# Attention bias made by distance, and full-height value weights, in a fused attention and expert kernel

## The chip, the cores and the metric

One core of a Trainium2 chip runs the whole program. The metric is device time in microseconds (us), a median over runs. PE is the matrix engine (TensorE), DVE VectorE, ACT ScalarE, POOL GpSimd, SP the engine that issues most DMAs.

## The reference, cut to what matters

```
scores = scale * q @ k^T                                  # 2 batches, 8 heads, 576 x 576, head_dim 64
psi_rel = log1p(|i - j|);  psi_i = log1p(max(i, 1))
x = psi_rel / psi_i
bias[h, i, j] = relu(x * w1 + b1) @ w2                    # 32 hidden units, 8 heads
attn = softmax(scores + bias)
x = attn @ v                                              # then reshaped to 1152 tokens x 512
x = sum_e p[e] * relu(x @ moe_w1[e]) @ moe_w2[e]          # 4 experts, 1024 wide
h = x @ w_in;  g = (a0+a1 h+a2 h^2+a3 h^3) / (1+|b0||h|+|b1|h^2 + 1e-6);  out = g @ w_out
```

For a given row i the bias depends on j only through |i - j|. All data are float32; a product is made from rounded high and low parts (the `h` and `l` tiles).

## The kernel before, in words

The program has three stages on one core: the bias (about 0 to 64 us), attention (to about 217 us), and the two expert stages. Within a stage, engines run their own queues in order and wait for each other on semaphores. DMA semaphores come in eight lanes, so a DMA waits for the one eight places ahead of it.

**Bias, `bias_phase`.** 36 groups `gg` of 16 rows each. A group has four tiles `q`; each is 128 partitions (4 rows x 32 hidden units) by 576 columns j. `hidden` (L402) makes each tile from a table of logarithms `ltab` (shifted by the row) and a per-partition constant `shift`: one instruction on DVE (L416) or ACT (L413), as `HIDDEN` says: "DDDA", three on DVE and one on ACT, 108 and 36 in all. `products` (L420) multiplies them on PE with `wm` in 32-column strips, two halves of 288 columns, into a PSUM tile `ps_ab` (3 buffers). `combine` (L436) divides by psi_i while it copies the PSUM tile on ACT into `bo` (L442), of which a tile holds a band of four groups (2 buffers); `store` (L426) writes a band to DRAM `bias_d`. `load_bias` (L492) reads 128 rows of two heads back for attention. Hidden tiles have 16 slots, four groups' worth, and run LEAD = 2 groups ahead of the products.

Between the groups stand other pieces: POOL splits k, q and v of head pair 0 into high and low (`split_hi` L527, `split_lo` L532) at the start, and k of the next at group 22; SP loads the next raw tiles behind the splits that free them; PE transposes k and q (`qk_T`, L548); at groups 34 and 35 the first two blocks of scores (L594) are already made.

**Attention.** Eight units n (head pair, batch), nine score blocks each. The order of all five queues is written by a small planner (`Flow`) from a table of costs and offsets (`CFG`). Per block: scores on PE (L594), bias and minimum on DVE (L608), exponent on ACT (L616), division on POOL (`norm`, L636), transposes on PE (L653, L666, L669), high and low copies on ACT and DVE (L678, L682). Per unit and half (256 or 320 rows) and head, `av` (L701) multiplies the transposed weights with v: for e = 0 to 3 a chunk of 128 keys, for e = 4 the last 64 keys. Both heads' last 64 keys lie in one v chunk and one tile `pe`, one head in partitions 0 to 63 and the other in 64 to 127, so e = 4 is a product over 64 partitions:

```
r = slice(64 * h, 64 * h + 64)
lh, rh = vs[r, 4].rearrange("p a d -> p (a d)"), el_[r, :W]
nc.tensor.matmul(ps[:, :W], lhsT=lh, rhs=rh, start=(e == 0 and m is mh), stop=(e == 4 and m is ml))
```

`pt_tiles` takes the weight tiles `pt` and `pe` from two buffers of 320 columns in turn, one half after the other.

Of the kernel before, what the change touches and what calls it, by code (L numbers as in the profile page):

```python
# [24 lines left out]
P = 128  # L25
# [14 lines left out]

NTQ, NDT = S // 4, 1148
LEAD = 2
# [3 lines left out]
EARLY = {34: (0,), 35: (1,)}  # L46
HIDDEN = ["DDDA"] * (S // 16)
OUT_DVE = ()

# [85 lines left out]
class Kernel:  # L135
# [16 lines left out]
    def run(self):  # L152
# [5 lines left out]
        self.dram = ctx.enter_context(self.pool("dscr", DRAM))  # L158
        self.bias_d = [self.dram.tile([P, H, S] if c < 4 else [16, H, 4, S], F32, name=f"bias_d{c}") for c in range(5)]
        self.nc.scalar.preload_act_table_set("natural_log_exp_and_others")  # L160
# [211 lines left out]


    def bias_phase(self):
        nc, t, pa = self.nc, self.t, self.pa
        cw = pa.tile([P, 10], F32, name="cw")
        mask = pa.tile([P, 4], F32, name="mask")
        shift = pa.tile([P, NTQ], F32, name="shift")
        rpsi = pa.tile([P, S // 16], F32, name="rpsi")
        ltab = pa.tile([P, NDT], F32, name="ltab")  # L380
        nc.sync.dma_start(out=cw, in_=t["w1_b1_w2"])
        nc.scalar.dma_start(out=shift, in_=t["c_psi"])
        for i, (a, b) in enumerate(((NDT - 640, NDT), (0, NDT - 640))):
            nc.sync.dma_start(out=ltab[:, a:b], in_=t["c_ltab"][:, a:b])
# [8 lines left out]
        nc.vector.tensor_scalar(out=shift, in0=shift, scalar1=b1, scalar2=None, op0=ALU.mult)  # L393
        nc.vector.tensor_scalar(out=ltab[:, NDT - 640:NDT], in0=ltab[:, NDT - 640:NDT], scalar1=w1, scalar2=None, op0=ALU.mult)
        wm = pa.tile([P, 4, H], F32, name="wm")
# [3 lines left out]

        NG = S // 16  # L400
        hid, outs, banks = {}, {}, {}
        hids = self.xpool.tile([P, 16, S], F32, tag="xa", bufs=1, name="hid")  # L402

        def hidden(gg):
            for q in range(4):
                if q % 2 == 0:
                    slot = (2 * gg + q // 2) % 8
                ht = hid[gg, q] = hids[:, 2 * slot + q % 2]
# [17 lines left out]
        def store(b):  # L426
            if b < 8:
                d = self.bias_d[b // 2][64 * (b % 2):64 * (b % 2) + 64].rearrange("(a q) h j -> (q h) a j", a=4)
            else:
                d = self.bias_d[4].rearrange("q h a j -> (q h) a j")  # L430
            nc.sync.dma_start(out=d, in_=outs[b])

        def combine(gg):
            b, G = divmod(gg, 4)
            if G == 0:
                outs[b] = self.wpool.tile([P, 4, S], F32, tag="we", bufs=2, name="bo")  # L436
            bo, ps = outs[b][:, G].rearrange("p (a b) -> p a b", a=2), banks.pop(gg)[:, :, 0:288]
            c = rpsi[:, gg:gg + 1]
            if gg in OUT_DVE:
                nc.vector.tensor_scalar(out=bo, in0=ps, scalar1=c, scalar2=None, op0=ALU.mult)  # L440
            else:
                nc.scalar.activation(out=bo, in_=ps, func=AF.Copy, scale=c)  # L442
            if G == 3:
                if b == 8:
                    self.bias_t[0, 4] = self.last_bias(outs[b].rearrange("(q h) a j -> h q a j", h=H))
                    self.last_band = lambda: store(b)
                else:
                    store(b)

        for gg in range(LEAD):  # L450
            hidden(gg)
        nc.vector.tensor_scalar(out=ltab[:, 0:NDT - 640], in0=ltab[:, 0:NDT - 640], scalar1=w1, scalar2=None, op0=ALU.mult)
        for nm in "kqv":
# [48 lines left out]
    def load_raw(self, n, nm):  # L502

        if n >= 8:
            return
        nc = self.nc
        p, b = n // 2, n % 2
        src = self.t[nm][b, 2 * p:2 * p + 2]  # L510
        r = self.front.tile([P, 9, D], F32, tag="raw" + nm, bufs=1, name="raw" + nm)
        if nm == "q":
# [11 lines left out]
    def split_hi(self, n, nm):  # L524
        nc, raw = self.nc, self.raw[n, nm]
        s = self.front.tile([P, 9, 2, D], F32R, tag="spl" + nm, bufs=(2 if nm == "v" else 1), name="spl" + nm)
        nc.gpsimd.tensor_scalar(out=s[:, :, 0, :], in0=raw, scalar1=1.0, scalar2=1.0, op0=ALU.mult, op1=ALU.mult)  # L527
# [37 lines left out]
    def attention_setup(self):  # L565
# [72 lines left out]
        def pt_tiles(n, half):  # L638
            if (n, half) not in PT:
                PT[n, half] = tuple(  # L640
                    (self.att.tile([P, 4, 2, 320], F32R, tag="pt" + x, bufs=2, name="pt" + x),
                     self.att.tile([P, 320], F32R, tag="pe" + x, bufs=2, name="pe" + x)) for x in "hl")
            return PT[n, half]
# [43 lines left out]
        def av(n, half, h, part):  # L687
# [6 lines left out]
            for e in ((0, 1), (2, 3, 4))[part]:  # L694
                for (m, el_) in ((mh, eh), (ml, el)):
                    if e < 4:
                        lh, rh = vs[:, 5 * h + e].rearrange("p a d -> p (a d)"), m[:, e, h, :W]
                    else:
# [546 lines left out]
def shape_consts():  # L1245
# [3 lines left out]
    g = np.repeat(np.arange(4), 32)  # L1249
    m = np.arange(NDT)  # L1250
    ltab = L[np.minimum(np.abs(m[None, :] - 572 - g[:, None]), S - 1)]
    r = 4 * np.repeat(np.arange(4), 32) + np.tile(np.repeat(np.arange(4), H), 4)
# [4 lines left out]
        "c_psi": np.ascontiguousarray(Pp[4 * np.arange(NTQ)[None, :] + g[:, None]]),  # L1257
        "c_rpsi": np.ascontiguousarray(rpsi),
        "c_ltab": np.ascontiguousarray(ltab),
    }  # L1260
# [23 lines left out]
```

## Time and profile before

| | |
|---|---|
| median of 3 runs | 808.53 us (808.22 to 809.11) |
| the profiled execution | 807.95 us, span 806.0 us |
| PE busy | 783.1 us (97%) |
| DVE / ACT / POOL busy | 649.4 / 488.3 / 455.0 us |
| granted PE clock, mean | 0.999 |

The span is what the trace covers; stretches of it are given by their start and end in us. An engine's busy time is the union of its instructions. A row of the timeline gives start, length, engine, line, operation, output<-inputs, shape and count; in brackets stand the idle time before it and what ended that. The duration of one instruction can reach past the start of the next on the same engine, so a repeated instruction's cost is taken as the distance of starts, or the length of a run of them by their number.

### The profile page before, as it was taken

To read this page: it belongs to the slowest core of one execution; us is meant where nothing else is said; L and a number is where in the kernel's file an instruction comes from. 1 tells how busy PE (TensorE), PEld (TensorE's weight loads), DVE (VectorE), ACT (ScalarE), POOL (GpSimd) and SP (SyncE) were. 2 spreads that over 40 slices of the span, in tenths; PEclk is the share of its full clock that TensorE was granted. 3 is DMA by queue.
4 is the path that set the end of the run, shared out by engine and by line. 5 is a ranking of instruction groups with operands and counts; after the bars stand their busy time and mean duration, and the time that the engine had idled before them with its cause. 6 is when DMAs were issued, how large, how long until landed. Compare 5 with 4: busy or idle time off the path is not lost.

```text
span 806.0 us, 13644 instructions
## 1 busy us (share of the span) xinstructions
PE 783.1 (97%) x4980; PEld 683.0 (85%) x4980; DVE 649.4 (81%) x1183; ACT 488.3 (61%) x932; POOL 455.0 (56%) x454
## 2 busy tenths in 40 slices
PE   6888999999999999999999999999999999999997
PEld 2337899988998999999999999999889889998986
DVE  7987888888687888878889878888678667888775
ACT  5898898889443334333333433333369998887772
POOL 3167689778346555444355545345166977754442
PEclk9999999999999999999999999999999999999999
DMA  5788747491013434432444333333130311000012
GB/s 127 264 284 229 196 104 201 105 233 54 1 30 102 131 131 129 137 116 93 147 139 144 131 105 119 117 131 105 40 105 27 119 64 53 1 0 1 1 40 78
DMA packets 67634, 87.37 MB, mean 108 GB/s; under 512 B 33520, under 2 KB 42096, under 8 KB 67440
## 3 DMA queue, kind: packets, MB, share of 16 engines
q1 hardware_dynamic: 66992, 86.35, 35.4%
q8 instruction: 39, 0.64, 0.3%
q14 instruction: 27, 0.22, 0.1%
q10 hardware_dynamic: 576, 0.16, 0.1%
HBM read 60.12 MB, written 21.36 MB: 101 GB/s over the span
## 4 chain that ended last, share of the span: by engine, by line
PE 77%; ACT 7%; POOL 6%; issue 4%; DVE 4%; DMA 2%; SPq 0%; POOLq 0%; DVEq 0%; ACTq 0%
PE ps_o L900 20%; PE ps_o L1150 11%; PE ps_y L992 10%; PE ps_h L1142 10%; PE ps_x L992 8%; PE ps L701 6%; PE ps L594 5%; PE ps L653 4%; ACT hid L413 2%; ACT bo L442 2%; POOL we L303 2%; PE ps_x L890 1%; PE ps L548 1%; POOL wml L303 1%; PE ps_y L890 1%
## 5 line engine op out<-in xcount | busy, mean ns | idle before, releaser
L900 PE MATMUL ps_o<-we,hs 128*128 128x512 f32 x810 | 203.4, 392 | 0.0
L900 PEld LDWEIGHTS ps_o<-we,hs 128*128 128x128 f32 x810 | 146.1, 188 | 25.8
L303 POOL TENSOR_TENSOR we<-wstg,we 128x512 fp32r<-128x512 f32 x40 | 57.0, 1446 | 130.3 <-ACT we L297 130.3
L906 DVE SCALAR_TENSOR_TENSOR acc<-ps_o,prob,acc 128x512 f32<-128x512 f32 x135 | 99.7, 743 | 30.1 <-PE ps_o L900 29.9
L1123 POOL TENSOR_TENSOR qq<-qq,ha 128x384 f32<-128x384 f32 x48 | 48.9, 1019 | 71.0 <-ACT qq L1120 71.0
L1150 PE MATMUL ps_o<-wmh,hs 128*128 128x512 f32 x252 | 83.5, 392 | 1.1 <-POOL hs L1134 1.1
L1142 PE MATMUL ps_h<-x,wmh 128*128 128x384 f32 x288 | 73.7, 337 | 0.0
L636 POOL TENSOR_SCALAR P<-P,ri 128x576 f32<-128x576 f32 x72 | 53.0, 747 | 33.3 <-DVE ri L627 18.8
L930 ACT ACTIVATE hs<-ps_x 128x576 fp32r<-128x576 f32 x32 | 20.8, 651 | 80.7 <-DVE ps_x L1004 74.0
L608 DVE CUSTOM_DVE_ANT_0 P<-ps,bias 128x576 f32<-128x576 f32 x72 | 53.6, 750 | 14.9 <-PE ps L594 12.9
L424 PE MATMUL ps_ab<-hid,wm 128*32 128x288 f32 x576 | 47.0, 425 | 12.0 <-DVE hid L416 7.5
L616 ACT ACTIVATE P<-P,nm 128x576 f32<-128x576 f32 x72 | 56.0, 780 | 3.3 <-DVE nm L608 3.1
L1129 DVE SCALAR_TENSOR_TENSOR qq<-qq,rr 128x384 f32<-128x384 f32 x48 | 26.6, 554 | 38.1 <-ACT rr L1128 35.1
L1150 PEld LDWEIGHTS ps_o<-wmh,hs 128*128 128x128 f32 x252 | 47.3, 188 | 11.4 <-POOL hs L1134 1.9
L328 POOL TENSOR_TENSOR wu<-wt,wu 128x512 fp32r<-128x512 f32 x28 | 36.2, 1314 | 36.4 <-ACT wu L324 36.4
L1142 PEld LDWEIGHTS ps_h<-x,wmh 128*128 128x128 f32 x288 | 52.6, 188 | 2.0
L682 DVE TENSOR_TENSOR ptl<-ps,pth 128x512 fp32r<-128x512 f32 x72 | 48.5, 683 | 5.2 <-ACT pth L678 4.7
L416 DVE TENSOR_SCALAR hid<-ltab,shift 128x576 f32<-128x576 f32 x108 | 52.6, 558 | 0.0
L594 PE MATMUL ps<-kh,qs 128*128 128x288 f32 x168 | 50.3, 321 | 1.4 <-DVE nm L608 1.3
L1134 POOL TENSOR_TENSOR hs<-pp,hs 128x384 fp32r<-128x384 f32 x48 | 48.9, 1019 | 3.5 <-issue 2.8
L424 PEld LDWEIGHTS ps_ab<-hid,wm 128*32 128x32 f32 x576 | 18.4, 112 | 37.0 <-ACT bo L442 13.9
L1150 PE MATMUL ps_o<-wml,hs 128*128 128x512 f32 x126 | 49.5, 393 | 0.0
(142 smaller groups left out, 2098.9 us busy)
## 6 DMA issues: line engine op xcount, KB each, us to landing
wstg<-moe_w SPq DMA_DIRECT2D x32, 512.0 KB, 3.7
bias_d<-bo SPq DMA_DIRECT2D x9, 1152.0 KB, 5.4
bias<-bias_d SPq DMA_DIRECT2D x16, 576.0 KB, 5.1
w<-moe_w_in SPq DMA_DIRECT2D x16, 512.0 KB, 4.4
w<-moe_w_out SPq DMA_DIRECT2D x16, 512.0 KB, 3.8
kl<-kh SPq DMA_DIRECT2D x16, 288.0 KB, 4.4
w_u<-wmag SPq DMA_DIRECT2D x16, 256.0 KB, 2.4
w_d<-wmag SPq DMA_DIRECT2D x16, 256.0 KB, 2.4
```

The lines of the kernel that those rows point to most:

```text
L303: nc.gpsimd.tensor_tensor(out=lo[:, sl], in0=stg[:, sl], in1=hi[:, sl].bitcast(F32), op=ALU.subtract)
L416: eng.tensor_scalar(out=ht, in0=d, scalar1=c, scalar2=0.0, op0=ALU.add, op1=ALU.max)
L424: nc.tensor.matmul(ps[32 * q:32 * q + 32, i, 0:288], lhsT=wm, rhs=hs[q][:, 288 * i:288 * i + 288], start=True, stop=True)
L594: nc.tensor.matmul(ps[:, half, dst:dst + w], lhsT=lhs, rhs=k[:, src:src + w], start=(i == 0), stop=(i == len(m) - 1))
L608: nc.vector.tensor_tensor_reduce(out=Pt[u][:, S * h:S * h + S].rearrange("p (a b) -> p a b", a=2), in0=ps[:, :, 0:288], in1=self.bias_t[n ...
L616: nc.scalar.activation(out=pt, in_=pt, func=AF.Exp, scale=-1.0, bias=stat.pop(g), accum_out=sums[n, c][:, h:h + 1])
L636: nc.gpsimd.tensor_scalar(out=pt[:, sl], in0=pt[:, sl], scalar1=ri, scalar2=1.0, op0=ALU.mult, op1=ALU.mult)
L900: nc.tensor.matmul(ps, lhsT=a, rhs=w[:, f, :], start=(f == i == 0), stop=(f == 1 and i == 2))
L906: nc.vector.scalar_tensor_tensor(out=acc[:, t], in0=ps, scalar=pr, in1=acc[:, t], op0=ALU.mult, op1=ALU.add)
L992: nc.tensor.matmul(ps[:, half, 0:288], lhsT=wu[:, w, i, k], rhs=x[v][:, k, 288 * half:288 * half + 288], start=(start and k == j == 0), st ...
L1142: nc.tensor.matmul(ps, lhsT=w[:, k, fo:fo + P], rhs=v[:, k, :], start=(k == i == 0), stop=(k == 3 and i == 2))
L1150: nc.tensor.matmul(ps, lhsT=a[:, P * tt:P * tt + P], rhs=w[:, f % 2, :], start=(f == i == 0), stop=(f == 3 and i == 2))
```

## The change

The change has four parts.

1. For groups 0 to 31 the bias is made by distance: a table `dtab` of log1p(d), d = 0, 1, ..., the same for every row, and only as many columns as the longest distance of the group, max(576 - 16 gg, 16 gg + 16). That is 576 columns at group 0, 304 at groups 17 and 18, 512 at group 31. The hidden tiles and the products have that width. `combine` writes the group twice from the same PSUM tile, the left part read backwards (columns 16 gg + 15 down to 1), the right part forwards, 591 columns in all. Groups 32 to 35 are made as before.
2. Each of these groups is stored by itself (32 stores instead of 8), into DRAM rows of 608, and `load_bias` reads them with a row step one element short, which puts each row's own shift in. Tiles of hidden units go "DDDD", "DDDD", "DDDA": 132 on DVE, 12 on ACT.
3. The raw v tile has ten chunks instead of nine: each head has its own chunk for its last 64 keys, the other half zero (written once). The product for e = 4 is over 128 partitions. v is loaded by four DMAs instead of one, and its two splits have 640 columns instead of 576.
4. The transposed weights have a tile for each half, of 256 and 320 columns, in one buffer each.

```
-HIDDEN = ["DDDA"] * (S // 16)
+HIDDEN = ["DDDD", "DDDD", "DDDA"] * (S // 48)
...
+        def width(gg):
+            return max(S - 16 * gg, 16 * gg + 16) if gg < NM else S
...
-                d, c = ltab[:, 572 - 4 * tt:572 - 4 * tt + S], shift[:, tt:tt + 1]
+                d, c = dtab[:, 0:width(gg)] if gg < NM else ltab[:, 572 - 4 * tt:572 - 4 * tt + S], shift[:, tt:tt + 1]
...
-            for i in range(2):
-                for q in range(4):
-                    nc.tensor.matmul(ps[32 * q:32 * q + 32, i, 0:288], lhsT=wm, rhs=hs[q][:, 288 * i:288 * i + 288], start=True, stop=True)
+            W = width(gg)
+            for i, (a, b) in enumerate(((0, min(W, 512)), (512, W)) if gg < NM else ((0, 288), (288, W))):
+                if b > a:
+                    for q in range(4):
+                        nc.tensor.matmul(ps[32 * q:32 * q + 32, i, 0:b - a], lhsT=wm, rhs=hs[q][:, a:b], start=True, stop=True)
...
+            b, G = divmod(gg, 4)
+            o = (P * ROW - 16) * (gg % 8)
+            d = self.bias_d[gg // 8].rearrange("q x -> (q x)")[o:o + P * ROW].rearrange("(p r) -> p r", r=ROW)
+            nc.sync.dma_start(out=d[:, 0:S + MARGIN], in_=outs[b][:, G])
...
+                m = 16 * gg + MARGIN
+                nc.scalar.activation(out=outs[b][:, G, 0:m], in_=ps[:, 1:m + 1][:, ::-1], func=AF.Copy, scale=c)
+                nc.scalar.activation(out=outs[b][:, G, m:], in_=ps[:, 0:S - 16 * gg], func=AF.Copy, scale=c)
+                store(gg)
...
-            self.nc.sync.dma_start(out=bt, in_=d[:, 2 * p:2 * p + 2])
+            o = MARGIN + 2 * p * ROW
+            d = d.rearrange("q x -> (q x)")[o:o + P * (H * ROW - 1)].rearrange("(q x) -> q x", q=P)[:, 0:2 * ROW]
+            self.nc.sync.dma_start(out=bt, in_=d.rearrange("q (h r) -> q h r", h=2)[:, :, 0:S])
...
+            for h in range(2):
+                nc.sync.dma_start(out=r[:, 5 * h:5 * h + 4], in_=rows[:, 5 * h:5 * h + 4])
+                nc.sync.dma_start(out=r[64 * h:64 * h + 64, 4 + 5 * h], in_=rows[64 * h:64 * h + 64, 4])
...
-                    if e < 4:
-                        lh, rh = vs[:, 5 * h + e].rearrange("p a d -> p (a d)"), m[:, e, h, :W]
-                    else:
-                        r = slice(64 * h, 64 * h + 64)
-                        lh, rh = vs[r, 4].rearrange("p a d -> p (a d)"), el_[r, :W]
+                    lh, rh = vs[:, 5 * h + e].rearrange("p a d -> p (a d)"), m[:, e, h, :W] if e < 4 else el_[:, :W]
```

On DVE the bias stage is one run of hidden tiles. Before, from the start of the program:

```order
L394 TENSOR_SCALAR ltab<-ltab,cw 128x640
L416 TENSOR_SCALAR hid<-ltab,shift 128x576 x6
L452 TENSOR_SCALAR ltab<-ltab,cw 128x508
L416 TENSOR_SCALAR hid<-ltab,shift 128x576 x12
L202 MEMSET one_eps 128x1
```

and now (the run goes on in the same manner, down to 304 columns and up again):

```order
L400 TENSOR_SCALAR dtab<-dtab,cw 128x576
L426 TENSOR_SCALAR hid<-dtab,shift 128x576 x4
L426 TENSOR_SCALAR hid<-dtab,shift 128x560 x4
L470 TENSOR_SCALAR ltab<-ltab,cw 128x640
L426 TENSOR_SCALAR hid<-dtab,shift 128x544 x3
L426 TENSOR_SCALAR hid<-dtab,shift 128x528 x4
L426 TENSOR_SCALAR hid<-dtab,shift 128x512 x4
L426 TENSOR_SCALAR hid<-dtab,shift 128x496 x3
L203 MEMSET one_eps 128x1
```

The first two groups are now wholly on DVE, and eight hidden tiles instead of six stand ahead of the second table's product; that product no longer stands between a tile and the table that the tile reads.

On SP, the loads of the second unit's k and v and the first stores, before (`rawk`, `rawv` raw tiles, `dp` the experts' shares):

```order
L517 DMA rawk<-k 128x9x64
L514 DMA rawq<-q 128x4x64
L515 DMA rawq<-q 64x1x64
L514 DMA rawq<-q 128x4x64
L515 DMA rawq<-q 64x1x64
L517 DMA rawv<-v 128x9x64
L198 DMA ab<-moe_a 128x4
```

and now:

```order
L548 DMA rawq<-q 64x1x64
L540 DMA rawv<-v 128x4x64
L541 DMA rawv<-v 64x64
L540 DMA rawv<-v 128x4x64
L541 DMA rawv<-v 64x64
L443 DMA bias_d_71<-bo 128x591 x3
L199 DMA ab<-moe_a 128x4
```

Three stores of groups now stand ahead of the eight small loads for the experts, and each load of v takes four places. In attention PE's queue has the same instructions in the same places as before.

## Rows read from the trace of the kernel before

**Rows 1.** The page: shares of the chain that ended last, by engine.

```profile
PE 77%; ACT 7%; POOL 6%; issue 4%; DVE 4%; DMA 2%; SPq 0%; POOLq 0%; DVEq 0%; ACTq 0%
```

**Rows 2.** Busy time by stretch: us, each engine's busy us (instructions), PE clock, DMA share, GB/s.

```profile
0.00:58.40 58.40, 46.49 (x562) 19.42 (x562) 54.27 (x116) 47.73 (x77) 22.41 (x15) 1.00 0.73 221
...
105.40:124.20 18.80, 18.79 (x142) 17.09 (x142) 15.84 (x50) 16.87 (x43) 16.07 (x24) 1.00 0.52 124
180.70:199.60 18.90, 18.65 (x134) 16.40 (x134) 16.05 (x51) 17.47 (x42) 17.69 (x22) 1.00 0.23 63
199.60:217.00 17.40, 17.40 (x121) 15.25 (x119) 12.64 (x35) 10.92 (x26) 6.66 (x11) 1.00 0.00 1
```

**Rows 3.** Matmuls of av in unit 6, head 1: timeline of PE; all 64-row ones by line.

```profile
204.83 0.31 PE L701 MATMUL ps<-pth,splv 128*128 128x320 f32 x1
204.98 0.30 PE L701 MATMUL ps<-ptl,splv 128*128 128x320 f32 x1
205.21 0.41 PE L701 MATMUL ps<-peh,splv 64*128 64x320 f32 x1
205.46 0.30 PE L701 MATMUL ps<-pel,splv 64*128 64x320 f32 x1
205.70 1.58 PE L653 MATMUL ps<-ident,P 128*128 128x128 f32 x12
...
L701 PE MATMUL ps<-peh,splv x32: 380/398/413, 77.6 to 216.5; 64*128 64x256 f32 x16, 64*128 64x320 f32 x16
```

**Rows 4.** Timeline of DVE, bias stage.

```profile
2.76 0.29 DVE L393 TENSOR_SCALAR shift<-shift,cw 128x144 f32<-128x144 f32 x1 [2.76 <-DMA shift<-c_psi]
4.37 0.55 DVE L394 TENSOR_SCALAR ltab<-ltab,cw 128x640 f32<-128x640 f32 x1 [1.32 <-DMA ltab<-c_ltab]
...
8.35 9.93 DVE L416 TENSOR_SCALAR hid<-ltab,shift 128x576 f32<-128x576 f32 x13
...
17.77 10.38 DVE L416 TENSOR_SCALAR hid<-ltab,shift 128x576 f32<-128x576 f32 x24
...
30.95 27.43 DVE L416 TENSOR_SCALAR hid<-ltab,shift 128x576 f32<-128x576 f32 x60
```

**Rows 5.** Timeline of POOL: the first split, and those of the second unit's k.

```profile
7.16 1.00 POOL L527 TENSOR_SCALAR splk<-rawk 128x576 fp32r<-128x576 f32 x1 [2.14 <-DMA rawk<-k]
...
38.07 12.76 POOL L527 TENSOR_SCALAR splk<-rawk 128x576 fp32r<-128x576 f32 x1 [6.56 <-PE ps L548]
50.91 1.49 POOL L532 TENSOR_TENSOR splk<-rawk,splk 128x576 fp32r<-128x576 f32 x1
```

**Rows 6.** ACT in the bias stage: groups by form, and one wait from its timeline.

```profile
L413 ACT ACTIVATE hid<-ltab,shift 128x576 f32<-128x576 f32 x36 | 29.3, 822 | 2.9 <-DVE ltab L394 2.9
L442 ACT ACTIVATE bo<-ps_ab,rpsi 128x576 f32<-128x576 f32 x36 | 28.3, 792 | 7.0 <-PE ps_ab L424 4.3 <-DMA bias_d<-bo 2.6
...
L195 ACT ACTIVATE identr<-ident 128x128 fp32r<-128x128 f32 x1 | 0.3, 298 | 0.0
...
25.71 0.74 ACT L442 ACTIVATE bo<-ps_ab,rpsi 128x576 f32<-128x576 f32 x1 [2.58 <-DMA bias_d<-bo]
```

**Rows 7.** Timeline, end of the bias stage: PE, DVE and ACT.

```profile
57.35 2.47 PE L424 MATMUL ps_ab<-hid,wm 128*32 128x288 f32 x32 [0.50 <-ACT bo L442]
...
60.58 0.76 DVE L608 CUSTOM_DVE_ANT_0 P<-ps,bias 128x576 f32<-128x576 f32 x1 [2.20 <-PE ps L594]
...
61.38 0.78 ACT L616 ACTIVATE P<-P,nm 128x576 f32<-128x576 f32 x1 [0.87 <-DVE nm L608]
...
63.99 0.72 ACT L442 ACTIVATE bo<-ps_ab,rpsi 128x576 f32<-128x576 f32 x1
...
64.76 0.71 PE L548 MATMUL ps<-identr,splk 128*128 128x128 f32 x6 [2.17 <-ACT bo L442]
```

**Rows 8.** DMA issues up to 100 us: KB each, median us to landing; timeline of SP.

```profile
bias_d<-bo SPq DMA_DIRECT2D x9, 1152.0 KB, 5.4
...
16.11 3.44 SPq L207 DMA_DIRECT2D dp<-moe_domain_probs  x6
```

More of the change, by code (lines that the diff above doesn't have):

```diff
@@ L38 @@
 W_MAX = f32_of_bits(0x47EFFFFF - (48 << 23))
-NTQ, NDT = S // 4, 1148
+NTQ, NDT = S // 4, 640
+ROW = 608
+MARGIN = 15
 LEAD = 2
@@ L158, in run @@
         self.dram = ctx.enter_context(self.pool("dscr", DRAM))
-        self.bias_d = [self.dram.tile([P, H, S] if c < 4 else [16, H, 4, S], F32, name=f"bias_d{c}") for c in range(5)]
+        self.bias_d = [self.dram.tile([P + 1, H * ROW] if c < 4 else [16, H, 4, S], F32, name=f"bias_d{c}") for c in range(5)]
         self.nc.scalar.preload_act_table_set("natural_log_exp_and_others")
@@ L379, in bias_phase @@
         rpsi = pa.tile([P, S // 16], F32, name="rpsi")
+        dtab = pa.tile([P, S], F32, name="dtab")
         ltab = pa.tile([P, NDT], F32, name="ltab")
@@ L382, in bias_phase @@
         nc.scalar.dma_start(out=shift, in_=t["c_psi"])
-        for i, (a, b) in enumerate(((NDT - 640, NDT), (0, NDT - 640))):
-            nc.sync.dma_start(out=ltab[:, a:b], in_=t["c_ltab"][:, a:b])
+        for i, (tab, nm) in enumerate(((dtab, "c_dtab"), (ltab, "c_ltab"))):
+            nc.sync.dma_start(out=tab, in_=t[nm])
             if i:
@@ L393, in bias_phase @@
         nc.vector.tensor_scalar(out=shift, in0=shift, scalar1=b1, scalar2=None, op0=ALU.mult)
-        nc.vector.tensor_scalar(out=ltab[:, NDT - 640:NDT], in0=ltab[:, NDT - 640:NDT], scalar1=w1, scalar2=None, op0=ALU.mult)
+        nc.vector.tensor_scalar(out=dtab, in0=dtab, scalar1=w1, scalar2=None, op0=ALU.mult)
         wm = pa.tile([P, 4, H], F32, name="wm")
@@ L407, in hidden @@
                     slot = (2 * gg + q // 2) % 8
-                ht = hid[gg, q] = hids[:, 2 * slot + q % 2]
+                ht = hid[gg, q] = hids[:, 2 * slot + q % 2, 0:width(gg)]
                 tt = 4 * gg + q
-                d, c = ltab[:, 572 - 4 * tt:572 - 4 * tt + S], shift[:, tt:tt + 1]
+                d, c = dtab[:, 0:width(gg)] if gg < NM else ltab[:, 572 - 4 * tt:572 - 4 * tt + S], shift[:, tt:tt + 1]
                 e = HIDDEN[gg][q]
@@ L437, in combine @@
             bo, ps = outs[b][:, G].rearrange("p (a b) -> p a b", a=2), banks.pop(gg)[:, :, 0:288]
[L438 to L448, printed above, removed]
+            nc.scalar.activation(out=bo, in_=ps, func=AF.Copy, scale=c)
+            if gg == NG - 1:
+                self.bias_t[0, 4] = self.last_bias(outs[b].rearrange("(q h) a j -> h q a j", h=H))
+                self.last_band = store_last
         for gg in range(LEAD):
             hidden(gg)
-        nc.vector.tensor_scalar(out=ltab[:, 0:NDT - 640], in0=ltab[:, 0:NDT - 640], scalar1=w1, scalar2=None, op0=ALU.mult)
+        nc.vector.tensor_scalar(out=ltab, in0=ltab, scalar1=w1, scalar2=None, op0=ALU.mult)
         for nm in "kqv":
@@ L510, in load_raw @@
         src = self.t[nm][b, 2 * p:2 * p + 2]
+        if nm == "v":
+            if n == 0:
+                self.rawv = self.front.tile([P, 10, D], F32, tag="rawv", bufs=1, name="rawv")
+                for h in range(2):
+                    nc.gpsimd.memset(self.rawv[64 - 64 * h:128 - 64 * h, 4 + 5 * h], 0.0)
+            r = self.rawv
+            rows = src.rearrange("h s d -> (h s) d").rearrange("(c p) d -> p c d", p=P)
+            for h in range(2):
+                nc.sync.dma_start(out=r[:, 5 * h:5 * h + 4], in_=rows[:, 5 * h:5 * h + 4])
+                nc.sync.dma_start(out=r[64 * h:64 * h + 64, 4 + 5 * h], in_=rows[64 * h:64 * h + 64, 4])
+            self.raw[n, nm] = r
+            return
         r = self.front.tile([P, 9, D], F32, tag="raw" + nm, bufs=1, name="raw" + nm)
@@ L525, in split_hi @@
         nc, raw = self.nc, self.raw[n, nm]
-        s = self.front.tile([P, 9, 2, D], F32R, tag="spl" + nm, bufs=(2 if nm == "v" else 1), name="spl" + nm)
+        s = self.front.tile([P, 9 + (nm == "v"), 2, D], F32R, tag="spl" + nm, bufs=(2 if nm == "v" else 1), name="spl" + nm)
         nc.gpsimd.tensor_scalar(out=s[:, :, 0, :], in0=raw, scalar1=1.0, scalar2=1.0, op0=ALU.mult, op1=ALU.mult)
@@ L639, in pt_tiles @@
             if (n, half) not in PT:
+                W = (256, 320)[half]
                 PT[n, half] = tuple(
-                    (self.att.tile([P, 4, 2, 320], F32R, tag="pt" + x, bufs=2, name="pt" + x),
-                     self.att.tile([P, 320], F32R, tag="pe" + x, bufs=2, name="pe" + x)) for x in "hl")
+                    (self.att.tile([P, 4, 2, W], F32R, tag=f"pt{x}{half}", bufs=1, name="pt" + x),
+                     self.att.tile([P, W], F32R, tag=f"pe{x}{half}", bufs=1, name="pe" + x)) for x in "hl")
             return PT[n, half]
@@ L1250, in shape_consts @@
     m = np.arange(NDT)
+    dtab = np.broadcast_to(L[None, :], (P, S))
     ltab = L[np.minimum(np.abs(m[None, :] - 572 - g[:, None]), S - 1)]
@@ L1258, in shape_consts @@
         "c_rpsi": np.ascontiguousarray(rpsi),
+        "c_dtab": np.ascontiguousarray(dtab),
         "c_ltab": np.ascontiguousarray(ltab),
```

17 lines of the change are left out of this document (10 added, 7 removed).

## The prediction

> **What bounds the kernel now.** I read the chain of waits first: 77% of it is PE, 7% ACT [rows 1]. Then the busy times by stretch [rows 2], which show two regimes. Up to 58.4 us, the bias stage, DVE is busy 54.3 of 58.4 us and ACT 47.7, PE 46.5. In attention PE is busy all the time (18.79 of 18.80 us in one unit, 17.40 of 17.40 at the end), but ACT (16.87) and POOL (16.07) are close behind. From 217 us on, nothing changes. So the bias edit is priced on DVE, the v edit on PE. The sum is made against the profiled execution, 807.95 us, which is 0.58 us under the median of 808.53; I carry the same difference over to the median.
>
> **Full-height value products: the main term.** The timeline of PE shows what the reader must see here: starts of `av`'s matmuls of 320 columns lie 0.15 us apart (204.83, 204.98), but from there to the first matmul over 64 partitions it is 0.23 us, to its partner 0.25, and to the next instruction over 128 partitions 0.24 [rows 3]. The three handovers take 0.72 instead of 0.45 us: 0.27 us are lost wherever one e = 4 pair stands. There are 32 of them [rows 3]. With 128 partitions the matmul has the shape of its neighbours, so I give it their distance: 32 x 0.27 = 8.6 us less on PE. The zeros cost nothing there, since a matmul's distance goes by its columns, which stay. Where the other head's product follows at once, its own first handover may get shorter too; by the same 0.10 us in some 12 places that would be 1.2 us more, which I keep for the lower end.
>
> Not all of it reaches the end. It is 1.1 us per unit. A unit of 18.8 us becomes 17.7; ACT needs 16.87, and POOL, whose two splits of v grow by a ninth, about 16.07 + 0.25 [rows 2]. In unit 6 ACT (17.47) and POOL (17.69 + 0.25) already meet the new 17.8 [rows 2]; in the last stretch neither is near. Three engines at 92 to 97% in queues whose order is fixed won't interleave without gaps, so I take seven eighths, **-7.5 us**, with the half and the whole as bounds. The tiles by half have the turn-taking of the two buffers before: nothing.
>
> **The bias stage: about the same work on DVE.** A hidden tile of 576 columns takes 10.38/24 = 0.43 us [rows 4]. The slope comes from two other scalar products: 0.55 us for 640 columns, 0.29 for 144, so 0.524 ns per column [rows 4]; that leaves 0.13 us per instruction whatever its width. Before: 108 x 0.43 = 46.4 us. Now 132 instructions of 58,416 columns together: 132 x 0.13 + 58,416 x 0.000524 = 47.5 us. The columns saved are given back by the 24 tiles that move over from ACT: **+1.1**. The bounds: if a tile costs 0.43 us at any width, 56.8 us (+10.4); if only columns count, 43.6 us (-2.8). I take the value between since the two rows of the same kind of instruction give it. The tables add 68 columns, under 0.1 us.
>
> POOL takes part in this. While it splits, DVE stands: 13 tiles from 8.35 us on took 9.93 us instead of 5.6 [rows 4], and the split of the second unit's k takes two of the last 60 tiles' places (27.43 - 60 x 0.43 = 1.6 us) [rows 4, 5]. Both stay; v's wider split adds a tenth of its two instructions, **+0.25**.
>
> ACT loses 24 tiles of 0.82 us [rows 6] and gains 32 second copies. A copy of 576 columns takes 0.79 us, one of 128 columns 0.30 [rows 6]: about 0.16 us each for no columns, 5 us together, plus 15 columns. Reading PSUM backwards is in no row. If it costs nothing, ACT falls to some 34 us; if each of the 8,416 columns so read cost twice its 1.1 ns, it is 43 us, still under DVE's. I take no cost; both ends are hidden by DVE.
>
> PE has 26% fewer columns and is hidden. SP issues 24 stores more, and six DMAs more for v ahead of them; an issue is 3.44/6 = 0.57 us [rows 8], so the first band is no earlier in DRAM than before. ACT's ninth copy waits 2.58 us for that band's landing [rows 6], as it may now; DVE is then up to four groups ahead, and it did not stop before. A store of a group moves a quarter of the 1152 KB that land in 5.4 us [rows 8].
>
> The end of the stage gets shorter. Before, the last tile ends at 58.4 us and attention's first transposes start at 64.76, held by ACT's last copy [rows 4, 7]: 6.4 us, since ACT was behind (PE waits for it at 57.35, DVE 2.20 us at 60.58 [rows 7]). With ACT free the path is one group of products (2.47/2 = 1.2 us), scores (0.7, from 59.8 to 60.58), bias 0.76, exponent 0.78, last copy 0.72 [rows 7]: 4.2 us, **-2.2**. If ACT were as late as before this would be 0. The stage: 1.1 + 0.25 - 2.2 = **-0.9**, rounded to -1.
>
> Sum: -7.5 - 1 = -8.5 us: 799.5 for a profiled execution, **800.0** for the median.
>
> **A rule on the shared port.** POOL's split of k at 38.07 us lasted 12.76 us, through some 28 boundaries between DVE's tiles, though its like takes 1.00 us at 7.16 [rows 5]: a gapless run of tiles keeps POOL out. The Trainium skill (SBUF — State Buffer, "Who interferes with whom") says that an engine that finds the port pair taken is blocked until the running instruction is finished, so at most one tile. By that rule the last rival below could not happen and has no chance; by the row it can, and the row decides.
>
> **The rivals.**
> - *The gain is lost in the queues.* For it: ACT and POOL at 90 and 85% of a unit [rows 2], all three queues fixed. Against: the chain names PE alone there. Half of 7.5, and nothing from the bias stage: 804.5 us.
> - *More comes out.* The handover after the pair goes as well (8.6 + 1.2 = 9.8 us, all of it), and k's split waits for the end of the tiles, where DVE has time (1.6 us), with the -1: 796 us. Against: ACT and POOL in unit 6.
> - *The product doesn't get faster.* If the slow handovers belong to the change of operand tiles (`pt` to `pe`), not to 64 partitions, they stay: 807.5 us. Against: neighbours also change between high and low tiles, at 0.15 [rows 3].
> - *Slower: POOL is kept out from the start.* Before, POOL's first split came in at 7.5 us, just where DVE went from tiles to the second table's product [rows 4, 5]. Now eight tiles run there, and no tile behind that product depends on it. If POOL is refused there, it gets in where DVE stops for a full set of slots, near 24 us. Behind the splits SP's queue holds the next raw tiles, the first stores and eight small loads, so the first band lands 16 us or so later and ACT's ninth copy with it; DVE can run four groups (5 us) ahead of that. Net about +11: 811 us. It decides only if the first split starts later than about 15 us; a start at the two memsets (14 us) costs 2 or 3 us.
>
> A lower granted clock of PE in the thinner bias stage is within the range: it was 1.00 throughout [rows 2], and even twice PE's time for its columns would stay near DVE's.
>
> **How the numbers follow.** A measurement of this kernel tells 0.2% (1.6 us) from no change. The forecast has 0.58 (797 to 803), the half 0.17, the more 0.12, no faster product 0.05, kept out 0.08. Faster: 0.58 + 0.17 + 0.12 = 0.87; same 0.05; slower 0.08. The range from 795 to 805.5 leaves out the last two cases, 0.13, and the outer edges of the others.
>
> **What would show it.** In the timeline after, the e = 4 matmuls stand at 0.11 and 0.15 us like the rest, and a unit takes 17.5 to 18 us. DVE's tiles end near 59.7 us, ACT has gaps in the bias stage, and attention's first transposes start near 63.8. Wrong would be: 0.2 us still around e = 4; units of 18.5 us with PE waiting for POOL or ACT; tiles of 0.4 us at 304 columns; a first split after 15 us; a copy read backwards that takes twice its length and holds PE.

## The result, and the profile after

The changed kernel takes **797.59 us** (median of 3 runs, 797.40 to 797.66) against 808.53: a ratio of 0.9862 (95% interval 0.9848 to 0.9877), 1.4% faster. The forecast was 800.0, with a range from 795 to 805.5. The profiled execution took 797.59 us as well (span 795.7). In a later set the same kernel took 796.53 (796.33 to 797.97) beside 808.79 before, a ratio of 0.9855 (0.9840 to 0.9870).

The chain of the page is what it was [rows 1]:

```profile
PE 76%; POOL 6%; ACT 6%; issue 5%; DVE 4%; DMA 2%; SPq 1%; ACTq 0%; POOLq 0%; DVEq 0%
```

Busy time by stretch, with the columns of [rows 2], for the bias stage, a unit, and the stretch of unit 6:

```profile
0.00:58.20 58.20, 49.10 (x355) 18.14 (x356) 53.97 (x140) 38.67 (x87) 29.86 (x15) 1.00 0.81 252
102.90:120.10 17.20, 17.20 (x142) 16.78 (x141) 15.82 (x50) 16.75 (x43) 16.76 (x23) 1.00 0.57 137
171.90:190.30 18.40, 17.52 (x134) 15.92 (x133) 16.50 (x52) 17.96 (x42) 17.48 (x22) 1.00 0.26 73
```

In the bias stage ACT is busy 38.7 of 58.2 us, no longer 47.7 of 58.4. A unit takes 17.2 us where it took 18.8. PE is still busy all of it, and ACT (16.75) and POOL (16.76) now run at 97% beside it. Only the stretch of unit 6 is no longer PE's: ACT works 17.96 of its 18.40 us, and that stretch fell by 0.5 us instead of 1.6.

The products of the values of unit 6, head 0, in the timeline of PE:

```profile
195.50 0.31 PE L731 MATMUL ps<-pth,splv 128*128 128x320 f32 x1
195.65 0.31 PE L731 MATMUL ps<-ptl,splv 128*128 128x320 f32 x1
195.79 0.31 PE L731 MATMUL ps<-peh,splv 128*128 128x320 f32 x1
195.94 0.31 PE L731 MATMUL ps<-pel,splv 128*128 128x320 f32 x1
196.09 1.03 PE L687 MATMUL ps<-ident,P 128*128 128x128 f32 x8
```

And the 32 products e = 4 of the high half by their line (durations, first and last start, forms):

```profile
L731 PE MATMUL ps<-peh,splv x32: 276/294/309, 76.9 to 206.2; 128*128 128x256 f32 x16, 128*128 128x320 f32 x16
```

The pair at 195.79 stands 0.15 us behind its neighbours and 0.15 us ahead of the next instruction, where [rows 3] had 0.23, 0.25 and 0.24. From the first to the last of these 32 starts it is 129.3 us; in [rows 3] it was 138.9. Attention gave back **9.6 us**. That is the net of two things, which the busy time over just these stretches shows, before and after:

```profile
77.60:216.50 138.90, 137.63 (x1019) 124.04 (x1018) 115.11 (x354) 119.17 (x292) 108.07 (x146) 1.00 0.52 133
76.90:206.20 129.30, 126.74 (x1018) 122.18 (x1018) 114.65 (x354) 119.15 (x292) 109.37 (x146) 1.00 0.54 141
```

PE is busy 10.9 us less, 0.34 us for each of the 32 pairs, and idle 2.6 us instead of 1.3: its waits for ACT grew from 0.5 to 1.0 us and those for POOL from nothing to 0.7.

The bias stage, DVE's timeline:

```profile
5.03 5.05 DVE L426 TENSOR_SCALAR hid<-dtab,shift 128x576 f32<-128x576 f32 x8
...
32.32 19.85 DVE L426 TENSOR_SCALAR hid<-dtab,shift 128x320 f32<-128x320 f32 x59
52.08 6.10 DVE L426 TENSOR_SCALAR hid<-ltab,shift 128x576 f32<-128x576 f32 x14
58.87 0.76 DVE L641 CUSTOM_DVE_ANT_0 P<-ps,bias 128x576 f32<-128x576 f32 x1 [0.69 <-PE ps L627]
```

POOL's timeline in the same stage:

```profile
7.15 1.06 POOL L560 TENSOR_SCALAR splk<-rawk 128x576 fp32r<-128x576 f32 x1 [2.06 <-DMA rawk<-k]
...
36.77 21.94 POOL L560 TENSOR_SCALAR splk<-rawk 128x576 fp32r<-128x576 f32 x1 [4.02 <-PE ps L581]
58.80 1.42 POOL L565 TENSOR_TENSOR splk<-rawk,splk 128x576 fp32r<-128x576 f32 x1
```

ACT's copies of results by line (busy us, mean ns, idle before), up to 64 us:

```profile
L457 ACT ACTIVATE bo<-ps_ab,rpsi 128x576 f32<-128x576 f32 (+31 forms) x32 | 18.4, 574 | 0.0
L456 ACT ACTIVATE bo<-ps_ab,rpsi 128x15 f32<-128x15 f32 (+31 forms) x32 | 16.5, 517 | 15.0 <-PE ps_ab L436 11.7 <-DMA bias_d<-bo 3.3
```

ACT's first wait for a store, from its timeline:

```profile
26.76 0.38 ACT L456 ACTIVATE bo<-ps_ab,rpsi 128x143 f32<-128x143 f32 x1 [1.83 <-DMA bias_d<-bo]
```

And the stores among the DMA issues up to 100 us (KB each, median us to landing):

```profile
bias_d<-bo SPq DMA_DIRECT2D x32, 295.5 KB, 4.3
```

DVE runs without a gap to 58.18 us (52.08 + 6.10). A tile of 576 columns takes 6.10/14 = 0.436 us; the 59 tiles of groups 16 to 31, 397 columns on average, take 0.336 each. POOL's first split came in at 7.15 us, in the midst of eight tiles, as early as before [rows 5]. Its split of the second unit's k was kept out for 21.94 us, to the end of the tiles, where it had been 12.76. ACT's copies read backwards (L456) cost no more than those read forwards (L457): the two means are over different widths, but of the 28 widths that both have, one column apart, they take 549 and 554 ns on average. A store of a group lands 4.3 us after its issue.

The end of the stage, in the timeline of PE:

```profile
60.51 0.37 PE L581 MATMUL ps<-identr,splk 128*128 128x128 f32 x3
63.05 0.71 PE L581 MATMUL ps<-identr,splk 128*128 128x128 f32 x6 [2.18 <-ACT bo L463]
```

In that of ACT:

```profile
59.67 0.78 ACT L649 ACTIVATE P<-P,nm 128x576 f32<-128x576 f32 x1 [2.09 <-DVE nm L641]
...
60.44 0.72 ACT L463 ACTIVATE bo<-ps_ab,rpsi 128x576 f32<-128x576 f32 x1
61.51 0.77 ACT L649 ACTIVATE P<-P,nm 128x576 f32<-128x576 f32 x1 [0.34 <-DVE nm L641]
...
62.28 0.72 ACT L463 ACTIVATE bo<-ps_ab,rpsi 128x576 f32<-128x576 f32 x1
```

And busy time by stretch, the granted clock behind the engines' columns:

```profile
60.90:63.00 2.10, 0.00 (x0) 0.00 (x0) 0.96 (x5) 1.76 (x5) 0.06 (x1) 1.00 0.85 236
64.50:68.00 3.50, 3.50 (x17) 3.47 (x17) 2.45 (x7) 2.17 (x5) 3.50 (x4) 0.51 0.84 171
```

From the last tile to attention's first transposes it is 4.9 us, against 6.4 before [rows 4, 7]; the transposes start at 63.05 instead of 64.76. The granted clock is 0.51 from 64.5 to 68 us, the lower of the two levels (1.2 GHz). PE had done nothing for 2.1 us up to 63.05 and had been at work again for 1.5 us when it fell. Before, the clock was 1.00 there, behind an idle time of the same length.

So the 10.4 us of the profiled execution are: -1.7 in the bias stage, +1.0 between its end and attention's first e = 4 product (12.84 us before, 13.85 after), and -9.6 in attention.

### The profile page after: what moved, and what is told of

It is laid out like the page before. It is cut to its first block, busy times and chain, and to the rows that moved or that the text cites. A ratio compares the mean times of both kernels' runs of the same rounds, so it can differ in the third digit from the quotient of the medians.

```text
span 795.7 us, 13247 instructions
## 1 busy us (share of the span) xinstructions
PE 774.5 (97%) x4756; PEld 680.7 (86%) x4756; DVE 647.8 (81%) x1207; ACT 477.1 (60%) x940; POOL 467.5 (59%) x456
## 4 chain that ended last, share of the span: by engine, by line
PE 76%; POOL 6%; ACT 6%; issue 5%; DVE 4%; DMA 2%; SPq 1%; ACTq 0%; POOLq 0%; DVEq 0%
PE ps_o L930 20%; PE ps_y L1022 10%; PE ps_o L1180 10%; PE ps_h L1172 9%; PE ps_x L1022 8%; PE ps L627 5%; PE ps L731 4%; PE ps L687 4%; POOL we L304 2%; PE ps_ab L436 1%; POOL wml L304 1%; PE ps_x L920 1%; DVE hid L426 1%; DMA bias_d<-bo 1%; PE ps L581 1%
## 5 line engine op out<-in xcount | busy, mean ns | idle before, releaser
L436 PE MATMUL ps_ab<-hid,wm 128*32 128x288 f32 (+18 forms) x352 | 48.1, 496 | 9.1 <-DVE hid L426 7.6
L1022 PEld LDWEIGHTS ps_y<-x,wu 128*128 128x128 f32 x336 | 47.5, 188 | 2.2
L1022 PEld LDWEIGHTS ps_x<-sums,wu 128*128 128x128 f32 x336 | 47.5, 188 | 2.2
```

Source lines behind the costliest of these rows:

```text
L436: nc.tensor.matmul(ps[32 * q:32 * q + 32, i, 0:b - a], lhsT=wm, rhs=hs[q][:, a:b], start=True, stop=True)
L1022: nc.tensor.matmul(ps[:, half, 0:288], lhsT=wu[:, w, i, k], rhs=x[v][:, k, 288 * half:288 * half + 288], start=(start and k == j == 0), st ...
```

## The experiments

### The shape of the last product

```diff
-    lh, rh = vs[:, 5 * h + e]..., m[:, e, h, :W] if e < 4 else el_[:, :W]
+    r = slice(0, P) if e < 4 else slice(64 * h, 64 * h + 64)
+    lh, rh = vs[r, 5 * h + e]..., m[:, e, h, :W] if e < 4 else el_[r, :W]
```

> The changed kernel with the last product of each head over 64 partitions again; all else of the change stays. Theory A (attention's gain is v's product over 128 partitions, by the spacing of the rows about 0.30 us for each of 32 pairs, 9.6 us in all): 806 to 807.5 us, a unit (first values' product of one half to that of the next unit) back from 17.2 to 18.8 us, the end of the bias stage where the changed kernel has it (attention's first transposes at 63.05 us). Rival B (attention got faster by the tiles by half or by another place in the queues, the product's shape counts little): below 801 us.

807.38 us (805.92 to 809.13, 10 runs); against before 0.9986 (0.9975 to 0.9996). The same group of products by its line:

```profile
L732 PE MATMUL ps<-peh,splv x32: 380/398/413, 76.0 to 214.9; 64*128 64x256 f32 x16, 64*128 64x320 f32 x16
```

From 76.0 to 214.9 it is 138.9 us again, to a tenth what it was before. PE's busy time in it is 137.63 us, as before. Theory A holds, B falls: the 9.6 us are the shape, net 0.30 us per pair. This run also shows what the change gives without the shape: about 1.1 us. It isn't the bias part alone, since v's four loads and its wider splits are still in it.

### The values' part alone

The kernel before with the ten blocks of v, the product over 128 partitions and the tiles by half; its bias as before.

> The kernel before with only the values' part of the change: ten blocks of v with zeros for the other head, the product over 128 partitions, tiles of transposed weights by half; bias as before. Theory A: attention gives its 9.6 us alone, 798.5 to 800 us, and the granted clock stays at 1.00 where attention starts, so that the bias part of the change is worth about 1.7 us less the 1 us that the fallen clock costs. Rival B (the bias part carries more than its stage shows, by what it leaves to attention): above 802 us.

801.94 us (800.87 to 802.23), ratio 0.9918 (0.9903 to 0.9933). That is neither theory's number: 6.5 us and not 9.6, 1.9 us above A's range and just under B's 802. Attention gave 8.6 (its e = 4 products lie between 80.7 and 211.0 us, 130.3 instead of 138.9). PE is busy 127.0 us of that, about as in the changed kernel, but idle 3.3 us and not 2.6; in the other traces with this product the same stretch takes 129.3 to 130.2 us. Ahead of attention 3.1 us were lost, since its first e = 4 product stood at 77.6 before. SP's timeline has the first store:

```profile
22.57 10.70 SPq L431 DMA_DIRECT2D bias_d<-bo  x3
```

ACT's has its longest wait:

```profile
27.78 0.74 ACT L442 ACTIVATE bo<-ps_ab,rpsi 128x576 f32<-128x576 f32 x1 [3.83 <-DMA bias_d<-bo]
```

PE's has attention's first transposes:

```profile
66.87 1.00 PE L560 MATMUL ps<-identr,splk 128*128 128x128 f32 x6 [2.18 <-ACT bo L442]
```

The store of the first band is issued at 22.57 us; before it was 19.65. Three more loads of v stand before it in SP's queue, and the eight small loads of the experts' constants: by SP's timeline the former are 1.7 us of the 2.9, the small loads took 0.8 longer than before, and the queue was 0.4 late from the start. ACT then waits 3.83 us for its landing, not 2.58 [rows 6], in a stage where ACT is full, and the transposes come at 66.87 and not 64.76. The other 1.0 us goes with the granted clock, which didn't stay at 1.00 as expected (0.63 from 66 to 68 us, 0.76 from 68 to 72). Gains don't add up here: without the shape the change gave 1.1 us, the values' part alone 6.5, all of it 10.9.

### Small loads behind the first store

```diff
-            if gg == 3:
+            if gg == 5:
                 self.setup_const()
```

One step moved, on top of the values' part alone:

> The values' part of the change alone, as in the run before, with one step moved: the eight small loads of the experts' constants (4.9 us of SP's queue) are issued behind the store of the first band, not ahead of it. Theory I (the values' part alone gained 6.5 us and not 9.6 because the three more loads of v in SP's queue put the first band's store 2.9 us later, from 19.65 to 22.57 us, for whose landing ACT waits 3.83 us): ACT's wait falls below 1 us, attention's transposes come at 64 to 65 us and not at 66.87, and the time is 1.5 to 3 us less: 799 to 800.5 us. Rival J (the stage is as long by DVE's tiles, which are gapless but for 0.42 us, and the 2 us come from the split of v and the fallen clock): within 0.7 us of 801.9.

798.05 us (796.71 to 798.98), ratio 0.9874 (0.9857 to 0.9890): 3.9 us less, more than theory I said: the transposes come 3.5 us sooner, where it had 2 to 3. The first store in SP's timeline:

```profile
17.69 0.38 SPq L431 DMA_DIRECT2D bias_d<-bo  x1
```

Attention's first transposes in PE's:

```profile
63.37 0.71 PE L560 MATMUL ps<-identr,splk 128*128 128x128 f32 x6 [2.18 <-ACT bo L442]
```

The store goes out at 17.69 us, ACT waits for no store at all in this stage, and the transposes come at 63.37. And on the kernel before, with nothing of the change:

> The kernel before with one step moved and nothing of the change: the eight small loads of the experts' constants go into SP's queue behind the store of the first band, not ahead of it. Theory I (ACT is full from 28 us on and its wait of 2.58 us for the landing of that store is on the path): the wait goes, attention's first transposes come at 62.2 to 62.8 us and not 64.76, 805.5 to 806.6 us. Rival J (DVE's gapless tiles hold the stage's length): within 0.7 us of 808.5.

807.35 us (805.98 to 807.60, 11 runs), ratio 0.9989 (0.9980 to 0.9998): 0.6 us less than before in its own set (807.91). That is above theory I's number, and the median alone would not refute J. In the trace ACT's wait is gone, and the transposes in PE's timeline come 1.6 us sooner than in [rows 7]:

```profile
63.12 0.71 PE L548 MATMUL ps<-identr,splk 128*128 128x128 f32 x6 [2.18 <-ACT bo L442]
```

Of these 11 runs, the three with a mean granted clock of 0.999 took 806.11 us on average, the eight with 0.997 or 0.998 took 807.40; for before in the same set it was 807.30 (9 runs) and 808.60 (8). At like clock it is 1.2 us, a comparison chosen after the runs; I's price of 1.9 to 3 us did not come. That the wait was on the path shows in the trace of before: the chain that ended last goes through the landing of that store and then through ACT, tile and copy in turn, up to 58.6 us:

```profile
19.65 5.97 DMA bias_d<-bo
...
25.71 0.74 ACT bo L442
26.45 0.67 ACT hid L413
...
57.96 0.64 ACT bo L442
```

There is one rival to rule out. In this run POOL's split of k came in only at the end of DVE's tiles (20.73 us from 36.68), so that DVE's last tile ended at 56.87 us, 1.5 us sooner than before. But the chain has no piece of DVE between 25.71 and 58.6 us before, and none between 26.07 and 56.9 us in this run; it is ACT's. With the wait gone the chain reaches ACT through PE's products at 26.07 us, and that leaves 1.6 of the 2.58 us. So the whole rewriting of the bias is worth about what moving one step is worth: both got the stage's end from 64.76 to 63.1.

### What the clock's fall costs

PE does the last group's eight products a second time, into the same results, in its idle time.

```diff
+            if gg == NG - 1:
+                last = [hid[gg, q] for q in range(4)]
...
             for g in EARLY.get(gg, ()):
                 self.scores(g)
+            if gg == NG - 1:
+                for i in range(2):
+                    for q in range(4):
+                        nc.tensor.matmul(banks[gg][32 * q:32 * q + 32, i, 0:288], lhsT=wm, ...)
```

> The changed kernel, but PE does the eight products of the last group twice: the second time (eight products, about 1.1 us) behind the scores of attention's second group, in its idle time before attention's transposes at 63.05 us; the results are the same. Theory C (the idle time of 2.18 us is what let the granted clock fall to 0.5 from 64.56 to 67.97 us, and that costs about 1 us): the granted clock stays at 1.00 there and the time is 0.7 to 1.2 us less, 796.4 to 796.9 us. Rival D (the clock falls anyway, or its fall is hidden by waits on DVE and ACT): within 0.3 us of 797.6, or later by the added 1.1 us where ACT comes to wait for the second set.

796.92 us (796.52 to 797.43), at the edge of theory C's range; the changed kernel's own later set, below, took 796.53, so this time by itself decides nothing. The transposes start at 62.95, and attention's start keeps its clock, in busy time by stretch:

```profile
64.50:68.00 3.50, 3.05 (x23) 2.58 (x21) 3.29 (x10) 2.92 (x7) 3.50 (x4) 1.00 0.82 169
```

Beside it, the changed kernel again:

> The changed kernel as it is, to see how often the granted clock falls where attention starts. Theory C (the fall to 0.5 costs 1.1 us whenever it comes): runs with a mean clock of 0.996 to 0.997 take about 1 us longer than those with 0.999 or 1.0, as attention's first values' product came at 75.62 us where it fell and at 74.53 us where it did not, with the same program up to there. Rival D (its cost is given back later): no relation of the two.

The clock fell in the profiled run (0.66 over 63 to 68 us) and that execution took 797.97 us; the two with a mean clock of 1.0 took 796.33 and 796.57, one with 0.998 took 796.49. Over both sets of the changed kernel: three runs at 0.999 or above average 796.8, four below it 797.4. But the first set alone shows little (797.40 at a mean clock of 1.0, 797.59 and 797.66 at 0.997 and 0.996). The clearest pair is the changed kernel and the run with the 64-row products, whose programs are the same up to attention's first values: PE idled 2.18 us ahead of the transposes in both, in the one the clock fell, in the other not, and the first product of the values started at 75.83 and 74.91 us (the 75.62 and 74.53 of the expectation stand in neither trace). The latter's transposes were 0.13 us later, so that is 1.05 us for 3.5 us at the lower level. So theory C holds for the cost in its place; that all of it comes through to the whole time isn't shown. The idle time alone doesn't decide whether the clock falls. With the second products, and in the next experiment with its shorter idle time, all eight runs stayed at 0.999 or above; of the 13 later runs with the shorter idle time two did not (0.998 and 0.996), and the one at 0.996 took 795.21 us beside 795.12 for two at 1.0. The Trainium skill (TensorE: Matmul & The Clock Gate, Part 1) says that the point at which the clock rises at a kernel's start differs from run to run; these runs show such a difference for a fall in the midst of a kernel.

### ACT's order at the end of the stage

```diff
             for g in EARLY.get(gg, ()):
                 self.biased(g)
+            for g in EARLY.get(gg - 1, ()):
                 self.exps(g)
```

> The changed kernel, but ACT takes the exponentials of attention's first two groups each one step later, behind the combines of groups 34 and 35 and not ahead of them. Theory E (the end of the bias stage, 4.9 us from the last tile to attention's transposes, is ACT's order: the combine of group 34 waits 2.09 us behind an exponential that waits for DVE, and the last combine sits behind the second one): attention's transposes at about 61.3 us and not 63.05, 1.7 us less, and with the shorter idle time no fall of the clock, 0.7 to 1 us more: 794.9 to 796 us. Rival F (what comes next is late anyway: the scores of the third group wait for DVE or for the copies of k): within 0.5 us of 797.6.

**795.63 us** (795.12 to 796.61), ratio 0.9844 (0.9829 to 0.9858). The transposes in PE's timeline:

```profile
61.07 0.71 PE L582 MATMUL ps<-identr,splk 128*128 128x128 f32 x6 [0.34 <-ACT bo L463]
```

PE waits 0.34 us for ACT's last copy, not 2.18; the transposes start 2.0 us sooner. By the time it is 0.9 to 2.0 us against the two sets of the changed kernel, and 1.0 us between the averages of the runs with a mean clock of 0.999 or above. Theory E holds: the last 2 us of the stage were two copies behind two exponentials in ACT's queue, which the change had left as they were.

### Is DVE the bound of the new bias stage?

The table of engines for the tiles, first with 12 more tiles on ACT, then with none there.

```diff
-HIDDEN = ["DDDD", "DDDD", "DDDA"] * (S // 48)
+HIDDEN = ["DDDD", "DDDA", "DDDA"] * (S // 48)
```

> The changed kernel, but ACT makes 24 tiles of the bias stage and not 12 (the last tile of two groups in three). Theory G (DVE's gapless run of tiles sets the stage's length: 132 tiles end at 58.18 us, about 0.40 us for each): 12 tiles less, DVE's last tile at about 53.4 us, and with ACT at 38.7 + 8.6 = 47.3 us of work in that time the end comes 3 to 4.8 us sooner: 793 to 794.7 us. Rival H (what stands behind DVE is as late: the stores and loads of the bias with a DMA share of 0.98 from 40 us on, or ACT, whose waits for landing stores cost 3.3 us): the last tile comes sooner, attention's first transposes do not, or by under 1.5 us: 796 to 798 us.

797.91 us (797.23 to 798.82), where the changed kernel in the same set took 796.53: nothing won, rival H. DVE's last tiles in its timeline:

```profile
50.18 5.67 DVE L426 TENSOR_SCALAR hid<-ltab,shift 128x576 f32<-128x576 f32 x13
```

POOL's split of k:

```profile
36.60 0.67 POOL L560 TENSOR_SCALAR splk<-rawk 128x576 fp32r<-128x576 f32 x1 [5.69 <-PE ps L581]
37.36 1.41 POOL L565 TENSOR_TENSOR splk<-rawk,splk 128x576 fp32r<-128x576 f32 x1
```

Attention's first transposes:

```profile
63.54 0.71 PE L581 MATMUL ps<-identr,splk 128*128 128x128 f32 x6 [2.18 <-ACT bo L463]
```

DVE's last tile ends at 55.85 us, 2.3 us sooner; the 12 tiles would have been 4.8. POOL's split got in at once here, and its 2.1 us are about what is missing. But the transposes come at 63.54, later than the 63.05 of the changed kernel: ACT, with 12 tiles more (some 8 us), is now behind: the chain that ended last goes through its tiles and copies and the landing of stores, for which it waits 2.9 us in all.

> The changed kernel, but DVE makes all 144 tiles of the bias stage. Theory G: 12 tiles more at 0.40 us, DVE's last tile at about 62.9 us and the time 4 to 5 us more, 801.6 to 802.6 us. Rival H (ACT or the stores are as much the bound, and ACT now has 8.5 us less to do): under 2 us more, below 799.6 us.

801.23 us (800.85 to 802.00): 3.6 to 4.7 us more than the changed kernel in its two sets, 0.4 us under theory G's range and far above rival H's. DVE's last tiles:

```profile
55.19 6.94 DVE L426 TENSOR_SCALAR hid<-ltab,shift 128x576 f32<-128x576 f32 x16
```

Attention's first transposes:

```profile
66.58 0.77 PE L581 MATMUL ps<-identr,splk 128*128 128x128 f32 x6 [1.91 <-ACT bo L463]
```

The last tile ends at 62.1 us, 3.9 later, and the transposes 3.5 later. Both ends together: DVE sets the stage, and ACT follows so closely that tiles moved from one to the other give nothing.

### Together

The changed kernel with ACT's order and the late small loads:

> The changed kernel with ACT's order as in the run that put the exponentials behind the last combines, and the eight small loads behind the first four groups' stores. Theory G (in the changed kernel DVE's gapless run sets the stage, so ACT's wait for a landing store, 1.8 to 3.3 us at 26 us, is slack): the time of the order alone, 795.1 to 796.2 us. Rival I (that wait is on the path here too): 793 to 794.5 us.

795.36 us (795.04 to 796.35), ratio 0.9846 (0.9833 to 0.9859): the order's time, as theory G said. The late loads give nothing on top. That ACT's waits for stores are slack here isn't shown by it: they only fell from 2.9 to 2.0 us. For theory G speaks that DVE's tiles end at 58.38 us, without a gap. With 24 tiles on ACT besides:

> The changed kernel with the order, the late small loads and 24 tiles on ACT. With 24 tiles alone DVE's last tile came 2.3 us sooner, at 55.85 us, and nothing was won, since ACT was behind. Theory M (ACT was behind by its 2.9 us of waits for landing stores): those go, attention's transposes come at 58.5 to 60 us, 793.2 to 795 us. Rival N (ACT's own work, some 47.5 us with its waits for PE, holds the end): no better than the order alone, 795.3 to 796.5 us.

795.16 us (795.12 to 797.15), between M's 795 and N's 795.3. ACT's waits for landing stores fell to 0.8 us. The transposes come at 60.52 us, 0.9 sooner than the 61.42 of the run without the 24 tiles, but not before 60, and attention's last products only 0.4 sooner: nearer to rival N, and not decided. And the old bias, with the values' part, the late loads and the order:

> The kernel before with the values' part, the late small loads and the exponentials behind the last combines, its bias made as before. If the bias by distance is worth little once the first band's store is not late (theory K): the 798.05 us of the run without the order, less the 1.5 to 2 us of the order: 796 to 796.6 us, at most 1 us behind the changed kernel with the same two steps. Rival L (ACT, full in the old bias stage, comes to hold the end as soon as the order is mended): above 797.3 us.

796.11 us (795.71 to 796.33), ratio 0.9851 (0.9839 to 0.9864): theory K. With both steps mended, the bias by distance is worth 0.75 us, and the two ranges overlap. The three versions of the changed kernel with ACT's order (795.16 to 795.63) stand 0.9 to 2.4 us ahead of the changed kernel itself; among the three these runs tell no difference.

## Why the prediction was right, and where it was not

**The main term, right in kind; its price was too small.** "32 x 0.27 = 8.6 us less on PE" measured 10.9: 0.34 us for each pair. The "next instruction" gains too, not in "some 12 places" and for the lower end only: where the other head's product follows, its first handover fell from 0.22 to 0.12 us (256 columns). The Trainium skill (TensorEngine Tiling (Array Packing), "Key Properties") says that a change of tiling mode drains TensorE. The rows agree for the steps into and out of the 64-row pair (0.23 and 0.24 us beside 0.15, [rows 3]). But the step inside the pair, where the shape stays, is as slow (0.25), so the change of shape isn't all of it; why that one is slow is open.

**"I take seven eighths" came out as a share.** Of the 10.9 us 9.6 reached the end, 0.88; the rest went to PE's longer waits for ACT and POOL. Half of that is in the stretch of unit 6, with ACT at 98% and PE idle 0.88 us instead of 0.25; in the other unit shown above ACT and POOL kept pace at 97%. So the forecast's -7.5 us was short by the price of a pair and not by the share.

**DVE's tiles, right.** "0.13 us whatever its width" and the slope held: 0.13 + 397 x 0.000524 = 0.338 us, and the 59 tiles of that mean width took 0.336. What failed was "Both stay": POOL's split of k waited for the end of the tiles, and the 1.6 us it had cost DVE went. Hence 58.18 us and not 59.7 for the last tile. ("26% fewer columns" on PE holds for groups 0 to 31; over all 36 it is 23%. PE is hidden there either way.)

**The end of the stage, right in sign.** 4.2 us were forecast, 4.9 measured. The working took one group's products and one chain of copies; it left out that ACT takes both exponentials ahead of the last copy. The two errors (-1.6 and +0.7) make the stage -1.7 where I had -0.9.

**The clock.** "A lower granted clock of PE in the thinner bias stage is within the range" put it in the wrong place. It fell behind the stage, after PE had had to wait, and cost 1.0 us in its place.

**The rivals.** The likeliest case was not the nearest. "More comes out" (796 us, chance 0.12) named both things that happened, the handover after the pair and the split that waits. That it came so near is in part luck: it had 9.8 us with nothing lost, where 10.9 came with 1.3 lost. The clock and 0.7 us at the stage's end kept the time above it. The working gave 799.5 for a profiled execution, and it took 797.59: 2.1 us more from attention and 0.8 more from the stage, less 1.0 for the clock. Of the two doubts that had been charged as costs, the loss in the queues was real and the split that stays was not. The slower rival did not come: POOL got in among tiles, at 7.15 us. So it needs no gap such as the second table's product, at which I had read it to get in before [rows 4, 5]. The rule of the Trainium skill (SBUF — State Buffer, "Who interferes with whom"), that the engine that comes second is blocked for the running instruction, would be a wait of at most one tile; that is again not what the row shows (21.94 us). Yet in the run with 24 tiles on ACT the split of the same k took 0.67 us as soon as its buffer was free, and with the order and the late loads besides, 12.14 us again. What decides is open.

**What the prediction did not see** is what held the old stage. It read ACT's 2.58 us wait for the first band's landing [rows 6] as something to be carried over. It was on the path: the store stood behind eight small loads in SP's queue. The chain through that store and ACT could have been read before. One moved step takes about the same time out of the old stage as all the new bias does (1.6 and 1.7 us).

## What to carry to other kernels

Where two shapes alternate on PE, read the spacing of the starts on both sides of the odd one, and one instruction further: the price is in the handovers. Zeros that make the shapes alike cost PE nothing here, since its starts lie 0.12 us apart at 256 columns and 0.15 at 320; what they cost in loads has to be looked for elsewhere. A forecast that multiplies a price by a share is checked on both: here the busy time of PE gives the price and its idle time the share. Before an engine's work is rewritten, look at what its longest wait stands behind in another engine's queue; moving that may give the same for one line. And the parts of a change need not add up: here one part's new loads cost the old bias stage 2 us, while in the new one DVE's tiles run without a gap beside them.

## What the hardware showed unexpectedly

- A copy on ACT that reads PSUM backwards costs no more: 549 ns on average over 28 widths from 79 to 511 columns (L456), 554 forwards at one column more (L457).
- POOL was kept out through a gapless run of DVE's tiles for 21.94 us; in one run with 12 tiles less on DVE it came in at once at about the same time (0.67 us at 36.60), in another it took 12.14 us.
- Two 64-row products in a row stand 0.25 us apart where 128-row ones of as many columns stand 0.15 apart.
- The granted clock fell 1.5 us after an idle time of PE of 2.1 us in one execution, and not after the same idle time in another; 3.5 us at the lower level cost 1.0 us in their place. Runs of before with a mean clock of 0.999 or above are 1.2 to 1.4 us faster than those below it (14 and 23 runs). Where it falls there, no trace shows.
